# Window attention with a sticky top-1 mixture of experts: first-layer matmuls over five PSUM banks, gathers and a branch hint issued at other places

## The chip, the cores and the metric

The kernel runs on one core of one Trainium2 chip. The core has five engines with an instruction queue each: TensorE (PE, with its weight loads listed as PEld), VectorE (DVE), ScalarE (ACT), GpSimd (POOL, which also issues the indirect DMAs here) and SyncE (SP, which issues the other DMAs). The metric is device time of one execution in microseconds (us); lower is better.

## The reference

Attention comes first: 8 batches, 8 heads, 512 local and 32 global positions. Its rows then go through a mixture of 8 experts. A token takes the expert with the largest logit, or, when its local gate is at least 0.5, the expert of the token before it.

```python
# attention, per batch and head (D = 64, window = 32)
out_g = sm(scale * q_g @ k_all.T) @ v_all                 # 32 global rows see everything
s_ll  = where(|i - j| <= 32, scale * q_l @ k_l.T, -1e9)   # 512 local rows see a band
out_l = sm([scale * q_l @ k_g.T, s_ll]) @ [v_g, v_l]      # and the 32 global keys
x = [out_g, out_l] as (8, 544, 512)
# experts (E = 8, F = 1024), token s of batch b
fresh = argmax(x[b, s] @ w_gate)
e = fresh if s == 0 or sigmoid(x[b, s] @ w_local) < 0.5 else e_of_previous_token
out[b, s] = softmax(x[b, s] @ w_gate)[e] * (relu(x[b, s] @ w1[e]) @ w2[e])
```

## The kernel before, in words

The program has three stretches. Until about 230 us it computes attention batch by batch and writes the rows x, with their gate values and token numbers, into a buffer `xs` in DRAM. From then on it computes experts, in blocks of rows that share one expert. Blocks 0 to 2 ("early", 256 rows each) use only rows of the first batches, and the end of attention and the routing of the last batches (the generator `tail`) run between their instructions. Blocks 3 to 10 ("rem") are one per expert and take what is left of it, in a number of rows known only at run time. Then come "full" blocks of 256 rows, each inside an `If`; three of them run with these inputs.

One block does this. Its rows are gathered from `xs` by indirect DMAs of 128 rows (`gather`, L1182, on POOL) into `xr4` (named `xa` in the trace), transposed on PE (`xpose`, L1196), and split by ACT (L1198) and DVE (L1199) into a high and a low part. The weights come in eight pieces of 128 x 1024 (`load`, L1135, on SP), and ACT (L1145) and DVE (L1155) split each piece in the same way. The first layer (`mm1`, L1242) makes eight groups fc = 0..7, each of 12 matmuls into one PSUM bank. ACT then takes the relu out of that bank (L1244), DVE takes the rest that ACT's rounding left (L1245), and only then is the bank free for another group. The second layer (`mm2`, L1253) adds up 24 matmuls of 512 columns for each 128 rows. `store` scales the result on ACT by a row factor (L1258) and scatters it by an indirect DMA on POOL (L1259). The row factors and token numbers are made on DVE by `scal` (L1208 to L1210), which reads all the gathered rows.

A rem block is a `Switch` over ten arms. Case 0 (`half`) takes 128 rows, with PE's operands exchanged. The other cases (`part`) take n = 256 to 512 columns in steps of 32. In `part` the first layer takes its banks from the ring `ph`, which holds three at that time. After the arm comes the common part, `close`: it stores the last result of the arm, runs the second layer for the last 128 rows, transposes the rows 256 to 511 of the next block, makes that block's scales, and gathers for the block after it. `xr4` is a single buffer, so each gather into it has to wait until `xpose` and `scal` have read what was there. The close of one block and the arm of the next transpose the rows of that next block: the arm the row groups 0 and 1, the close the groups 2 and 3.

Before a Switch a `hint` is issued on every engine: it loads the case number from `cnd` (L1420) and announces the branch (L1426). For the first rem block this stands in early block 2. The case numbers are the last eight small DVE operations of `kinds` (L1048 to L1064). The row lists of the first rem block come from the first `pick`: three DVE operations (L989 to L993), 34 small matmuls on PE (L999), two DVE operations (L1001, L1002), then its four gathers. `pick` waits a number of turns of `tail` between its DVE operations and its matmuls; one turn in two falls to a hook after a group of matmuls.

All engines run in program order, and the order of the program is that of the Python code: `hook` and `step`, called after each group of matmuls, put one or more pieces of the other engines' work at that place.

Of the kernel before, what the change touches and what calls it, by code (L numbers as in the profile page):

```python
# [30 lines left out]
NT = 34  # L31
# [7 lines left out]
NX = 3  # L39
# [550 lines left out]
class Route:  # L590
# [414 lines left out]
    def lists(self, po):  # L1005
        nc = self.nc
        yield from self.place(self.cntp, NT, NX, NR)
        cid = self.tmp("cid", [P, 2 * E + NR, 2], BF16)
# [19 lines left out]
        phi = self.tmp("phi", [P, NT], BF16)  # L1028
# [4 lines left out]
        for c0 in range(CA, NT, 5):  # L1033
            yield from self.low(c0, min(c0 + 5, NT))
        self.pk = (cid, phi)
        yield from self.pick(cid, phi, self.o2, 0, 4, 2 * NX, ((0, NT),), po, 12)

    def kinds(self):
        nc = self.nc
# [31 lines left out]
class Moe:  # L1071
# [100 lines left out]
        e = self.rt.eide[0:1, i:i + 1] if i < NX else self.rt.eid[0:1, i - NX - E:i - NX - E + 1]  # L1172
        return self.nc.sync.value_load(e, min_val=0, max_val=E - 1)

    def gather(self, i):
        if i >= NSLOT:
            return
        k = self.kind(i)
        src = self.xs[0:P * (CA + 1)] if k == "early" else self.xs
        c0 = 2 * i if k == "early" else 2 * NX + 4 * (i - NX) if k == "rem" else 2 * NX + 4 * E + 2 * (i - NX - E)  # L1180
        for j in range(4 if k == "rem" else 2):
            self.nc.gpsimd.indirect_dma_start(out=self.xr[j] if k == "early" else self.xr4[:, j], out_offset=None, in_=src,  # L1182
                                              in_offset=bass.IndirectOffsetOnAxis(ap=self.rt.idx[:, c0 + j:c0 + j + 1], axis=0))

# [44 lines left out]
            self.load()  # L1229
            self.split(True)  # L1230

    def mm1(self, i, fc, xh, xl, hh, hl, n0, n1):
        nc = self.nc
        hi, lo = self.wp[8 * i + fc // 2]
        hi = hi.rearrange("p (c f) -> p c f", c=4)
        lo = lo.rearrange("p (c f) -> p c f", c=4)
        fs = slice(P * (fc % 2), P * (fc % 2) + P)
        ph = self.ph()[:, 0:n1 - n0]
        n = 0
        for a, b_ in ((hi, xh), (lo, xh), (hi, xl)):  # L1240
            for dc in range(4):
                nc.tensor.matmul(ph, a[:, dc, fs], b_[:, dc, n0:n1], start=(n == 0), stop=(n == 11))  # L1242
                n += 1
        nc.scalar.activation(out=hh[:, fc, n0:n1], in_=ph, func=AF.Relu)  # L1244
        nc.vector.scalar_tensor_tensor(out=hl[:, fc, n0:n1], in0=ph, scalar=0.0, in1=hh[:, fc, n0:n1].bitcast(F32), op0=ALU.max, op1=ALU.subtract)  # L1245
# [50 lines left out]
    def early(self, i):  # L1296
# [4 lines left out]
        for fc in range(8):  # L1301
            self.mm1(i, fc, *x, 0, 256)
            self.hook(i, fc)
        self.ph = Ring(self.ph.t[0:n])
        py = self.py()
        for fc in range(8):
# [5 lines left out]
                    self.gather(i + 2)  # L1312
        if mid:
            self.widen()
            self.finish(True)
        self.store(py, 0)
        py = self.py()
        for fc in range(8):
            if mid and fc == 1:
                while not self.known:  # L1320
                    self.take(next(self.tail))
                self.hint(i + 1)
            self.mm2(i, py, fc, 1, *x[2:])
            self.hook(i, 16 + fc)
            if mid and fc in XPM:
                self.xpose(i + 1, XPM.index(fc))
                if fc == XPM[-1]:
                    self.scals(i + 1)
# [45 lines left out]
    def part(self, i, n0, n1, groups):  # L1374
# [2 lines left out]
            for t in self.g:  # L1377
                self.nc.vector.tensor_copy(t[:, 1:2], t[:, 3:4])
        for fc in range(8):
            self.mm1(i, fc, *x, n0, n1)  # L1380
            self.step(fc % 2 == 0, fc != 4)
        for g, j in enumerate(groups):
            last = j == groups[-1] and self.kind(i) == "rem"
# [11 lines left out]
    def close(self, i, j):  # L1395
        py = self.py.t[j % 2]
        if self.kind(i) == "rem":
            self.store(self.ps[7], 1)
        for fc in range(8):
            self.mm2(i, py, fc, j, self.HH, self.HL)  # L1400
            if fc in (2, 5):
                self.xpose(i + 1, 2 + fc // 3)
                if fc == 5:
                    self.scals(i + 1)
                    self.gather(i + 2)
            self.step(fc in (1, 3, 5, 7))
        self.store(py, j)

# [145 lines left out]
```

## Time and profile before

| | us |
|---|---|
| median of three runs | 718.87 |
| lowest, highest | 712.88, 720.37 |
| the profiled execution, whole | 717.19 |
| its span, first to last instruction | 715.4 |
| PE busy | 674.5 (94% of the span) |
| DVE busy | 426.9 (60%) |
| ACT busy | 343.7 (48%) |
| POOL busy | 199.3 (28%) |
| mean granted PE clock | 0.979 |

PE is busy for all but a few places, so what counts is where it stands still and where its granted clock is low. A row of the waits names who waited, who ended it, the sum of the time, the number of times and the longest. A row of the timeline has the start, the duration of the merged group, the engine, line and operation, the tiles written and read, and in brackets the idle time before it and what ended that.

The second and third early block begin their first layers at 268.1 and 296.0 us. The rem blocks begin their arms at 327.3 (480 columns), 372.0 (`half`), 392.8 (352), 433.3 (448), 476.5 (352), 511.3 (288), 543.1 (448) and 586.6 (416). The full blocks begin at 628.0, 651.5 and 674.9.

### The profile page before, as it was taken

The page shows a single profiled execution, that of the slowest core. Times are in us where ns is not written, and L with a number is a line of the kernel's source. Part 1 is how long each engine was busy: PE and PEld are TensorE (multiplying, and loading weights), DVE is VectorE, ACT ScalarE, POOL GpSimd, SP SyncE. Part 2 cuts the span into 40 slices and gives each one's busy share as a digit, 9 for nine tenths or more (in the row PEclk, how much of TensorE's full clock was granted, in tenths as well). Part 3 has the DMA queues.
Part 4 walks back from the last instruction along what each step waited for, and adds up shares of the span by engine and source line. Part 5 has one row for each costly group of instructions (what it writes and reads, how often), then busy time and mean ns, then how long its engine had stood idle before and what let it go on. Part 6 is the DMA issues. An engine that isn't in the chain of part 4 may idle for free. (4 is left out here: it accounts for less than half of the span.)

```text
span 715.4 us, 18380 instructions
## 1 busy us (share of the span) xinstructions
PE 674.5 (94%) x7253; PEld 565.9 (79%) x7253; DVE 426.9 (60%) x1057; ACT 343.7 (48%) x614; POOL 199.3 (28%) x321
## 2 busy tenths in 40 slices
PE   8999999999899999898997799999999999999990
PEld 7777777777677869787886789889888889899880
DVE  7878777778887777893335526335445325166550
ACT  4565555555546646453345435243535334256550
POOL 6634434343343110412023213031303020122201
PEclk9999999999999999999998899999999999999996
DMA  8966876966585676767327727246556326176551
GB/s 330 371 244 238 325 276 236 356 252 224 219 309 178 222 231 234 258 212 279 96 95 260 252 82 239 94 137 212 172 191 206 121 90 198 65 264 236 194 194 50
DMA packets 42869, 150.92 MB, mean 211 GB/s; under 512 B 7950, under 2 KB 9230, under 8 KB 38545
## 3 DMA queue, kind: packets, MB, share of 16 engines
q1 hardware_dynamic: 35392, 126.39, 50.6%
q0 software_dynamic: 6960, 21.90, 8.9%
q8 instruction: 77, 1.26, 0.7%
q14 instruction: 152, 1.24, 0.6%
q10 hardware_dynamic: 288, 0.13, 0.1%
HBM read 130.02 MB, written 19.69 MB: 209 GB/s over the span
## 5 line engine op out<-in xcount | busy, mean ns | idle before, releaser
L1253 PE MATMUL ps<-wp,wq 128*128 128x512 f32 x504 | 128.1, 401 | 0.5 <-ACT wq L1353 0.5
L1259 POOL DMA_INDIRECT out_dram<-y,tk x39 | 48.0, 1232 | 287.7 <-ACT y L1258 259.7
L1242 PE MATMUL ps<-wp,wp 128*128 128x256 f32 (+5 forms) x672 | 110.8, 325 | 3.5 <-issue 2.5
L1242 PEld LDWEIGHTS ps<-wp,wp 128*128 128x128 f32 x672 | 105.0, 191 | 8.9 <-issue 3.9
L1253 PEld LDWEIGHTS ps<-wp,wq 128*128 128x128 f32 x504 | 93.7, 191 | 20.5 <-ACT wq L1353 0.9
L1199 DVE TENSOR_TENSOR wp<-ps,wp 128x512 fp32r<-128x512 f32 x40 | 27.5, 690 | 106.9 <-ACT wp L1198 106.8
L1245 DVE SCALAR_TENSOR_TENSOR wq<-ps,wq 128x256 fp32r<-128x256 f32 (+5 forms) x80 | 41.9, 526 | 80.3 <-ACT wq L1244 67.7
L1244 ACT ACTIVATE wq<-ps 128x256 fp32r<-128x256 f32 (+5 forms) x80 | 37.3, 468 | 84.7 <-PE ps L1242 79.1
L191 POOL TENSOR_SCALAR_AFFINE_SELECT qbd<-raw 64x512 f32<-64x512 f32 x62 | 44.6, 720 | 118.1 <-PE ps L243 98.1
L243 PE MATMUL ps<-kx,qbd 128*64 128x128 f32 x1024 | 70.8, 280 | 0.9 <-issue 0.7
L243 PEld LDWEIGHTS ps<-kx,qbd 128*64 128x64 f32 x1024 | 54.7, 137 | 11.9 <-issue 7.8
L1182 POOL DMA_INDIRECT xa<-xs,idx x42 | 46.6, 1110 | 59.9 <-issue 41.8
L1258 ACT ACTIVATE y<-ps,pp 128x512 f32<-128x512 f32 x39 | 26.9, 690 | 72.9 <-PE ps L1253 66.4
L248 DVE TENSOR_REDUCE mx<-ps 128x4 f32<-128x512 f32 x64 | 43.9, 686 | 26.8 <-PE ps L243 26.7
L1155 DVE TENSOR_TENSOR wp<-raw,wp 128x1024 fp32r<-128x1024 f32 x47 | 57.1, 1217 | 0.0
L254 ACT ACTIVATE pe<-pe 128x512 f32<-128x512 f32 x64 | 40.7, 636 | 30.3 <-DVE pe L250 30.3
L1145 ACT CAST wp<-raw 128x1024 fp32r<-128x1024 f32 x49 | 51.1, 1046 | 4.2 <-DMA raw<-in_w_dram 3.4
L1198 ACT CAST wp<-ps 128x512 fp32r<-128x512 f32 x40 | 23.5, 588 | 58.1 <-PE ps L1196 58.0
L250 DVE TENSOR_TENSOR pe<-ps,mx 128x512 f32<-128x512 f32 x64 | 44.0, 688 | 1.6
L276 PE MATMUL ps<-v,pt 128*32 128x65 f32 x2048 | 42.4, 222 | 2.4 <-DVE xa L284 0.8
L276 PEld LDWEIGHTS ps<-v,pt 128*32 128x32 f32 x2048 | 33.3, 110 | 13.8 <-issue 6.6
L191 POOL TENSOR_SCALAR_AFFINE_SELECT kx<-raw 128x384 f32<-128x384 f32 (+3 forms) x127 | 42.8, 369 | 2.8 <-DMA raw<-in_qk_dram 0.7
(287 smaller groups left out, 1173.3 us busy)
## 6 DMA issues: line engine op xcount, KB each, us to landing
raw<-in_w_dram SPq DMA_DIRECT2D x79, 512.0 KB, 4.3
v<-in_vw_dram SPq DMA_DIRECT2D x32, 1040.0 KB, 9.3
raw<-in_qk_dram SPq DMA_DIRECT2D x32, 528.0 KB, 7.1
xa<-in_w_dram SPq DMA_DIRECT2D x22, 512.0 KB, 4.2
xT<-in_w_dram SPq DMA_DIRECT2D x22, 512.0 KB, 5.7
xs<-xa SPq DMA_DIRECT2D x8, 1056.0 KB, 4.6
qgb<-in_qg_dram SPq DMA_DIRECT2D x8, 128.0 KB, 4.0
xa<-xs,idx POOLq DMA_INDIRECT x42, 5.8
```

Source lines behind the costliest of these rows:

```text
L191: self.nc.gpsimd.affine_select(out=out, in_=in_, pattern=pat, compare_op=ALU.is_ge, fill=0.0, base=0, channel_multiplier=0)
L243: nc.tensor.matmul(sp[64 * t2:64 * t2 + 64, t], qbd[:, w], kf[:, f:f + P], start=False, stop=True, skip_group_check=True)
L248: nc.vector.tensor_reduce(out=mx, in_=st["sp"], axis=AX.X, op=ALU.max)
L250: nc.vector.tensor_tensor(out=st["pe"][:, 4 * hb:4 * hb + 4], in0=st["sp"], in1=mx.broadcast_to([P, 4, P]), op=ALU.subtract)
L276: nc.tensor.matmul(o[32 * w4:32 * w4 + 32, g, h], pt[:, 2 * g + w4 // 2, w4 % 2, h, :], v[:, w, h * (D + 1):(h + 1) * (D + 1)], start=True ...
L1145: nc.scalar.copy(out=hi, in_=raw)
L1155: (nc.gpsimd if pool else nc.vector).tensor_tensor(out=lo, in0=raw, in1=hi.bitcast(F32), op=ALU.subtract)
L1182: self.nc.gpsimd.indirect_dma_start(out=self.xr[j] if k == "early" else self.xr4[:, j], out_offset=None, in_=src, in_offset=bass.IndirectO ...
L1242: nc.tensor.matmul(ph, a[:, dc, fs], b_[:, dc, n0:n1], start=(n == 0), stop=(n == 11))
L1245: nc.vector.scalar_tensor_tensor(out=hl[:, fc, n0:n1], in0=ph, scalar=0.0, in1=hh[:, fc, n0:n1].bitcast(F32), op0=ALU.max, op1=ALU.subtract)
L1253: nc.tensor.matmul(py, a[:, fc, js], b_[:, fs], start=(fc == 0 and k == 0), stop=(fc == 7 and k == 2))
L1259: sc = nc.gpsimd.indirect_dma_start(out=self.out, out_offset=bass.IndirectOffsetOnAxis(ap=self.g[1][:, j:j + 1], axis=0), in_=y, in_offset ...
```

## The change

Four things change.

1. In `part`, the first layer takes the banks 2, 3, 6, 1, 7, 2, 3, 6 for its groups 0 to 7, where it took 2, 3 and 6 in turn.
2. In `close`, the row scales of the next block and the first two gathers for the block after it stand behind the first group of the second layer (they stood behind the sixth); the transposes stand behind the groups 2 and 4 (2 and 5), and the other two gathers behind group 4.
3. The matmuls of the first `pick` come ten turns of `tail` later (a wait of 22 for 12), which is five groups of the first layer of early block 2: they stood ahead of its group 0 and stand ahead of its group 5.
4. In early block 2, `finish(True)`, what is left of `kinds`, and the first hint stand behind the last group of the first layer. `finish(True)` stood behind the second layer's first 128 rows, the rest one group later.

```diff
@@ lists @@
-        yield from self.pick(cid, phi, self.o2, 0, 4, 2 * NX, ((0, NT),), po, 12)
+        yield from self.pick(cid, phi, self.o2, 0, 4, 2 * NX, ((0, NT),), po, 22)
@@ gather @@
-    def gather(self, i):
+    def gather(self, i, part=range(4)):
...
-        for j in range(4 if k == "rem" else 2):
+        for j in part:
+            if j >= 2 and k != "rem":
+                break
@@ mm1 @@
-    def mm1(self, i, fc, xh, xl, hh, hl, n0, n1):
+    def mm1(self, i, fc, xh, xl, hh, hl, n0, n1, bank=None):
...
-        ph = self.ph()[:, 0:n1 - n0]
+        ph = (self.ph() if bank is None else bank)[:, 0:n1 - n0]
@@ early @@
         for fc in range(8):
             self.mm1(i, fc, *x, 0, 256)
             self.hook(i, fc)
+            if mid and fc == 7:
+                self.finish(True)
+                while not self.known:
+                    self.take(next(self.tail))
+                self.hint(i + 1)
...
         if mid:
             self.widen()
-            self.finish(True)
         self.store(py, 0)
         py = self.py()
         for fc in range(8):
-            if mid and fc == 1:
-                while not self.known:
-                    self.take(next(self.tail))
-                self.hint(i + 1)
             self.mm2(i, py, fc, 1, *x[2:])
@@ part @@
-            self.mm1(i, fc, *x, n0, n1)
+            self.mm1(i, fc, *x, n0, n1, self.ps[(2, 3, 6, 1, 7, 2, 3, 6)[fc]])
@@ close @@
-            if fc in (2, 5):
-                self.xpose(i + 1, 2 + fc // 3)
-                if fc == 5:
-                    self.scals(i + 1)
-                    self.gather(i + 2)
+            if fc == 0:
+                self.scals(i + 1)
+                self.gather(i + 2, (0, 1))
+            if fc in (2, 4):
+                self.xpose(i + 1, 1 + fc // 2)
+                if fc == 4:
+                    self.gather(i + 2, (2, 3))
```

The first place is PE's queue in early block 2 around the hint (`cnd` holds the case numbers, `ps_63` and `ps_64` are the banks of the second layer, `ps_65` and `ps_66` banks of the first; behind L1244 and L1255 of the changed kernel stand L1242 and L1253 of the kernel before). Before:

```order
L1253 MATMUL ps_63<-wq_4315,hl 128x512
L1253 MATMUL ps_64<-wq_4314,hh 128x512 x2
L1253 MATMUL ps_64<-wq_4314,hl 128x512
L1420 TENSOR_LOAD cnd
L1426 SWITCH_STRIDE
L1426 ISA
L1426 BRANCH_PREFETCH_HINT
```

After:

```order
L1244 MATMUL ps_65<-xl,wp_4313 128x256 x4
L1244 MATMUL ps_66<-xh,wp_4313 128x256 x8
L1244 MATMUL ps_66<-xl,wp_4313 128x256 x4
L1424 TENSOR_LOAD cnd
L1430 SWITCH_STRIDE
L1430 ISA
L1430 BRANCH_PREFETCH_HINT
L1255 MATMUL ps_63<-wq_4314,hh 128x512 x2
```

The four instructions of the hint have moved from behind nine groups of the second layer to the place between the two layers.

The second place is DVE's queue at the end of the first layer of early block 2 (`hl<-ps` frees a bank of the first layer, `wp<-raw,wp` is a split of weights, `kq`, `kb` and `kt` lead to the case numbers in `cnd`). Before:

```order
L1155 TENSOR_TENSOR wp_100<-raw_77,wp_100 128x1024
L1245 SCALAR_TENSOR_TENSOR hl<-ps_65,hh 128x256
L1055 TENSOR_SCALAR kb<-kq 1x8
L1058 TENSOR_SCALAR kt<-kq 1x8
L1060 TENSOR_TENSOR kt<-kt,kb 1x8
L1245 SCALAR_TENSOR_TENSOR hl<-ps_66,hh 128x256
L1062 SCALAR_TENSOR_TENSOR kt<-left,kt 1x8
L1064 TENSOR_TENSOR cnd<-kt,kb 1x8
L1155 TENSOR_TENSOR wp_101<-raw_78,wp_101 128x1024
L1245 SCALAR_TENSOR_TENSOR hl<-ps_63,hh 128x256
```

After:

```order
L1155 TENSOR_TENSOR wp_4207<-raw_79,wp_4207 128x1024
L1247 SCALAR_TENSOR_TENSOR hl<-ps_66,hh 128x256
L1048 TENSOR_SCALAR kq<-cn 1x8
L1050 TENSOR_SCALAR kq<-kq 1x8
L1052 TENSOR_SCALAR kq<-kq 1x8
L1055 TENSOR_SCALAR kb<-kq 1x8
L1058 TENSOR_SCALAR kt<-kq 1x8
L1060 TENSOR_TENSOR kt<-kt,kb 1x8
L1062 SCALAR_TENSOR_TENSOR kt<-left,kt 1x8
L1064 TENSOR_TENSOR cnd<-kt,kb 1x8
L1424 TENSOR_LOAD cnd
```

The last eight operations of `kinds` stood spread between the groups 2 to 4; they now stand together behind the last group, with the hint right behind them.

The third place is DVE's queue in the common part of the first rem block (`tm_99`, `tk_96` and `pp_93` are the scales and token numbers of the next block, `wp_4311<-ps` the low parts of its transposed rows). Before:

```order
L1420 TENSOR_LOAD cnd
L1426 SWITCH_STRIDE
L1426 ISA
L1426 BRANCH_PREFETCH_HINT
L1199 TENSOR_TENSOR wp_4311<-ps_68,wp_4209 128x4x128
L1155 TENSOR_TENSOR wp_4207<-xa_109,wp_4207 128x1024
L1155 TENSOR_TENSOR wp_4208<-xa_109,wp_4208 128x1024
L1199 TENSOR_TENSOR wp_4311<-ps_67,wp_4209 128x4x128
L1208 TENSOR_TENSOR tm_99<-xa_108,eoh 128x32
L1209 COPY tk_96<-xa_108 128x4
L1210 TENSOR_REDUCE pp_93<-tm_99 128x4
```

After:

```order
L1424 TENSOR_LOAD cnd
L1430 SWITCH_STRIDE
L1430 ISA
L1430 BRANCH_PREFETCH_HINT
L1210 TENSOR_TENSOR tm_99<-xa_108,eoh 128x32
L1211 COPY tk_96<-xa_108 128x4
L1212 TENSOR_REDUCE pp_93<-tm_99 128x4
L1201 TENSOR_TENSOR wp_4311<-ps_68,wp_4209 128x4x128
L1155 TENSOR_TENSOR wp_4207<-xa_109,wp_4207 128x1024
L1201 TENSOR_TENSOR wp_4311<-ps_67,wp_4209 128x4x128
L1155 TENSOR_TENSOR wp_4208<-xa_109,wp_4208 128x1024
```

The three operations of the scales have moved ahead of everything that DVE does with this common part's transposes. POOL's queue keeps its order (store of the arm's last rows, four gathers, store of the common part).

## The prediction

> **What bounds the kernel now.** I read first the page, then PE's waits from 290 us on, because nothing before that is moved, then the timelines around each wait. The page gives the span; PE is busy in nearly all of it.
>
> ```profile
> span 715.4 us, 18380 instructions
> ```
>
> The waits of PE from 290 us to the end, longest sum first:
>
> ```profile
> PE ps L1242 <- DVE wq L1245: 3.9, 2, 3.6
> PE ps L999 <- DVE xT L993: 3.3, 1, 3.3
> PE ps L1196 <- DMA xa<-xs,idx: 3.2, 2, 2.3
> PE ps L1242 <- issue: 2.5, 1, 2.5
> PE ps L1242 <- ACT wp L1145: 0.9, 1, 0.9
> PE ps L1196 <- DVE wp L1199: 0.8, 1, 0.8
> PE ps L1253 <- ACT wq L1353: 0.5, 1, 0.5
> ```
>
> Together they are 15.1 us, and the change aims at three of them: the bank wait of the first layer (3.9), the first pick (3.3), the gathers of the rows after `half` (3.2). The granted clock adds to them. The 3 us behind the wait at the first pick, in the table of stretches (PE, PEld, DVE, ACT and POOL busy, granted clock, share and rate of the DMA engines):
>
> ```profile
> 296.00:299.00 3.00, 3.00 (x19) 3.00 (x16) 2.42 (x4) 0.10 (x1) 2.18 (x2) 0.51 0.91 280
> ```
>
> PE is busy all the time, at half clock. So a standstill of about 3 us costs itself and a slow stretch behind it.
>
> **Early block 2: the first pick and the hint.** PE's timeline there:
>
> ```profile
> 295.10 1.00 PE L999 MATMUL ps<-xT,o 128*128 128x8 bf16 x34 [3.27 <-DVE xT L993]
> 295.96 1.99 PE L1242 MATMUL ps<-xh,wp 128*128 128x256 f32 x8
> ...
> 300.41 1.12 PE L1242 MATMUL ps<-xh,wp 128*128 128x256 f32 x8
> ...
> 309.05 0.62 PE L1253 MATMUL ps<-wq,hh 128*128 128x512 f32 x2
> ```
>
> The six groups 2 to 7 of the first layer run from 300.41 to 309.05, 1.44 us each. Groups 0 and 1 took 4.45 (295.96 to 300.41) where they take 2.88, so the slow clock cost 1.6 us. With the pick gone from ahead of group 0, PE could begin at 295.10 - 3.27 = 291.8. What is late next is DVE:
>
> ```profile
> 294.70 3.49 DVE L1155 TENSOR_TENSOR wq<-raw,wq 128x1024 fp32r<-128x1024 f32 x3
> ...
> 303.16 0.32 DVE L1048 TENSOR_SCALAR kq<-cn 1x8 int32<-1x8 int32 x1
> ...
> 303.79 1.21 DVE L1155 TENSOR_TENSOR wp<-raw,wp 128x1024 fp32r<-128x1024 f32 x1
> ...
> 305.26 0.15 DVE L1055 TENSOR_SCALAR kb<-kq 1x8 f32<-1x8 int32 x1
> ...
> 305.60 0.41 DVE L1245 SCALAR_TENSOR_TENSOR hl<-ps,hh 128x256 fp32r<-128x256 f32 x1
> ```
>
> In its queue three weight splits stand ahead of the first L1245, and they run until 298.2 whatever PE does. The early blocks keep three banks, so groups 0 to 2 run from 291.8 to 296.1 and group 3 waits until 298.2 + 0.4 = 298.6. Of the 3.27 us, 2.5 return as a bank wait. Then groups 3 and 4 end at 301.5, the pick (0.9, from 295.10 to 295.96) at 302.4, groups 5 to 7 at 306.7, where before they ended at 309.05: 2.3 us won.
>
> But now the hint stands here, and PE loads the case number that DVE must first make. Group 6 ends at 305.3; relu and L1245 (0.2 + 0.4 + 0.4) bring 306.3, three small operations 306.6, the split that now stands ahead of group 7's L1245 (1.2) 307.8, that L1245 308.2. The eight operations of the case numbers took 0.63 us for the first three (303.16 to 303.79), 0.34 for the next three (305.26 to 305.60) and about 0.3 for the last two: `cnd` at 309.5. The relu's 0.4 is that of this row, which begins 0.2 after PE:
>
> ```profile
> 309.25 0.39 ACT L1244 ACTIVATE hh<-ps 128x256 fp32r<-128x256 f32 x1 [1.05 <-PE ps L1242]
> ```
>
> No row shows a hint on an empty PE queue. Its price lies between 0 (before, it was hidden among the matmuls) and the 2.5 that PE spent at the first Switch with nothing to wait for (its wait "issue"). I take 0.5, PE's wait at L1253 after `half`, where a jump and a hint also stand behind a drained queue. So the second layer begins at 310.0, 1.0 later than before. PE has then stood for 3.3 us, and I count one stretch at half clock, 1.6 us as after the old wait. That lets DVE catch up, so its 0.8 at L1196 goes: +1.8 us by the first Switch. The 2.5 there I leave as it is: the 34 short matmuls still drain PE's queue right before it, and how much an announcement 15 us ahead instead of 9 helps is shown nowhere (0 to 2.5 won). Bounds of the whole place: -2.8 (hint free, no half clock, Switch wait gone) and +7.4 (hint 2.5, half clock after both standstills, 1.6 and 2.9, the latter the dearest in the trace, from the next part). I stay in the middle because of PE's two standstills one, 2.5 us, is shorter than the old 3.27, and the other, 3.3, as long.
>
> [...]
>
> The first gathers start about 4 us later than before (after L1002 at about 303, which was at 298.3), but their rows are needed first at 318; they took 6 us, so 0.
>
> **The block after `half`.** PE, ACT, DVE and POOL:
>
> ```profile
> 384.37 4.10 PE L1253 MATMUL ps<-wp,wq 128*128 128x512 f32 x9 [0.52 <-ACT wq L1353]
> ```
>
> ```profile
> 378.95 1.06 ACT L1145 CAST wp<-raw 128x1024 fp32r<-128x1024 f32 x1
> ...
> 389.68 0.69 ACT L1258 ACTIVATE y<-ps,pp 128x512 f32<-128x512 f32 x1 [5.35 <-DMA out_dram<-y,tk]
> ```
>
> ```profile
> 380.72 0.69 DVE L1199 TENSOR_TENSOR wp<-ps,wp 128x512 fp32r<-128x512 f32 x1
> ```
>
> ```profile
> 373.46 1.35 POOL L1182 DMA_INDIRECT xa<-xs,idx  x1 [5.67 <-PE ps L1362]
> ...
> 380.14 1.42 POOL L1259 DMA_INDIRECT out_dram<-y,tk  x1 [0.31 <-ACT wp L1145]
> ```
>
> `half` is short, and the gathers, issued from 373.46 on, land after PE wants them. With the scales first on DVE the first two gathers are issued 5.4 us earlier, when the store ahead of them is done (about 368), and both waits of L1196 end. But the win is not 3.2 us plus the rest: ACT is busy with a weight cast until 380.0 and takes the first transposed rows only then, DVE's part of them begins at 380.72 and ends at 381.4, and the last transposes of `half` need their bank. They can start at about 381.5; with 0.9 for them and ACT's copy, the second layer begins at 382.4 instead of 384.37: -2.0. PE still stands mostly idle ahead of that, so I leave the slow clock (up to 1.8 more if it goes: nine matmuls took 3.9 us here, and 2.1 at 0.234 each, a third of 0.70, the usual group of three).
>
> Then the next first layer, of 352 columns:
>
> ```profile
> 392.83 4.08 PE L1242 MATMUL ps<-wp,hh 128*128 128x352 f32 x24
> 396.75 2.08 PE L1242 MATMUL ps<-wp,hl 128*128 128x352 f32 x12
> 402.47 3.89 PE L1242 MATMUL ps<-wp,hl 128*128 128x352 f32 x12 [3.64 <-DVE wq L1245]
> 406.15 9.00 PE L1242 MATMUL ps<-wp,wp 128*128 128x352 f32 x48
> ```
>
> ```profile
> 401.89 0.52 DVE L1245 SCALAR_TENSOR_TENSOR wq<-ps,wq 128x352 fp32r<-128x352 f32 x1 [5.06 <-issue]
> ```
>
> DVE reaches this arm at 396.8 (401.89 - 5.06) and stands 5.06 us with nothing that the profile shows to wait for; I take it for code that isn't there yet. PE fills three banks and stops. Five banks carry PE to 392.8 + 5 x 1.96 = 402.6, and DVE frees the first at 402.4 (401.89 + 0.52). Besides, the store at 380.14, which waited behind four gathers, goes out near 374, so ACT's 5.35 at the `y` buffer shrinks, and DVE gets through the common part sooner. Either alone nearly ends the stop. The layer took 22.3 us (392.83 to 406.15 + 9.00); 96 matmuls at the pace of the first 24, 3.92 us, are 15.7: -6.6, of which 3.6 is the wait and 2.9 the slow clock behind it. Bounds: -2.0 for the whole part (DVE's code later still, the stop returns) and -10.4.
>
> The other arms never waited for a bank but for 0.2 us (516.5 us): -0.2. Bank 7 is read by the store at the beginning of the common part and bank 1 by one at its end, 0.7 us long; groups 4 and 3 come at least 4.3 us (three groups) later, so the new banks cost 0; if ACT came later than that, PE would wait for what is left.
>
> **The end.** POOL issues the last two gathers, which nobody needs, ahead of the last store:
>
> ```profile
> 698.48 0.69 ACT L1258 ACTIVATE y<-ps,pp 128x512 f32<-128x512 f32 x1 [1.07 <-PE ps L1253]
> ```
>
> ```profile
> 700.83 1.02 POOL L1259 DMA_INDIRECT out_dram<-y,tk  x1 [0.30 <-issue]
> ```
>
> Now they start when the store before them is out (694.9) and need 2.6 us, so the last store starts 0.4 after `y`, at 699.5: -1.3 (between -0.5 and -1.5). In the other common parts POOL has 4 to 25 us of slack; the moved scales, transposes and gathers cost 0 under PE's 24 matmuls. Were DVE to wait there for a late gather, the transposes behind the scales would be late with it.
>
> **Sum.** +1.8 - 2.0 - 6.6 - 0.2 - 1.3 = -8.3. The profiled execution took 717.19 (span 715.4), so 708.9. It lies 1.7 below the median of the runs shown, 718.87, so against that median the forecast is -1.4%.
>
> **Rivals.** About 1% is what a measurement of this kernel can tell from no change.
>
> *The cover is not there (25%).* DVE's 5 us without a reason are no fault of the gathers; if the shorter `half` gives the hint less time before the Switch, DVE comes later by as much as PE wins. Then the part is worth -2.0, the sum -1.7, the time 715. For it: ACT's waits have "issue" too, behind other Switches. Against it: five banks and an earlier DVE both have to fail.
>
> *The hint stops PE (7%), slower.* `cnd` may come later than 309.5, since each of the splits ahead needs its weights: a landing 2.4 us later than the usual 4.2 (the slowest load of that stretch took 6.6) moves it to 311.9; a hint on an empty queue as dear as DVE's 5.06 moves the second layer to 317.0; with 2.9 for the clock that is +10.9, less 0.8. With the part after `half` at its -2.0 and the end at -1.3 the time is 724. It decides for slower once early block 2 loses more than the 10 us that the other parts win; against it, that no PE row shows more than 2.5 without a reason.
>
> *It pays in full (8%).* No half clock at either place, and the earlier hint ends the 2.5: -2.8 - 10.4 - 0.2 - 1.3 = -14.7, 702.5.
>
> The forecast itself has 60%. The predicted time is 709, and the forecast's own range 705 to 712. For 8 in 10 I take 704 to 717. Faster by over 1% (under 711.7) are the forecast nearly whole and the full pay: 0.64. Within 1%: 0.29. Slower: 0.07.
>
> **What would show it.** Right: L999 in early block 2 without a wait and instead about 2.5 us of PE waiting for L1245 at group 3; PE idle about 3 us between the layers with the case numbers ending it; no wait of L1196 for a gather in `half`; no wait for a bank in the block behind it, even if DVE still stands without a reason; the last store within 0.5 us of its `y`. Wrong: a PE wait of over 4 us at the hint, or the bank wait still there with five banks, or new PE waits in the common parts of the eight rem blocks.

## The result, and the profile after

The changed kernel takes 711.12 us (median of 13 runs, 709.32 to 715.48), the kernel before in the same series 717.33 us (13 runs). The ratio is 0.9916, with a 95% interval of 0.9892 to 0.9941: 0.84% faster, where 1.4% was forecast. That 1.4% was taken against 718.87, the median of three runs; against 717.33 the predicted 709 us is 1.2% less. The profiled execution took 711.1 us with a span of 709.4, 6.0 less than before.

These are PE's waits from 285 us on in the changed kernel, longest sum first. The lines are numbered two higher than before (L1255 is the second layer, L1244 the first, L1198 the transposes):

```profile
PE ps L1255 <- issue: 4.1, 1, 4.1
PE ps L1244 <- DVE hl L1247: 2.5, 1, 2.5
PE ps L1353 <- DVE wp L1201: 1.1, 1, 1.1
PE ps L1255 <- ACT wq L1355: 1.0, 1, 1.0
PE ps L1244 <- issue: 0.7, 1, 0.7
PE ps L1244 <- ACT wp L1145: 0.7, 1, 0.7
PE ps L1198 <- DVE wq L1356: 0.6, 1, 0.6
```

All three waits that the change aims at are gone (3.9, 3.3 and 3.2 us). Two new ones stand at the top, both in early block 2.

**Early block 2.** PE's timeline: the beginning of the first layer, its fourth group (group 3), the first pick, the beginning of the second layer, the second pick and the first arm:

```profile
293.57 1.12 PE L1244 MATMUL ps<-xh,wp 128*128 128x256 f32 x8
...
300.52 1.22 PE L1244 MATMUL ps<-xh,wp 128*128 128x256 f32 x8 [2.48 <-DVE hl L1247]
...
304.70 1.10 PE L999 MATMUL ps<-xT,o 128*128 128x8 bf16 x34
...
314.27 1.22 PE L1255 MATMUL ps<-wq,hh 128*128 128x512 f32 x2 [4.05 <-issue]
...
331.95 8.37 PE L1244 MATMUL ps<-wp,wp 128*128 128x480 f32 x38 [0.67 <-issue]
```

The first layer begins at 293.57, 1.74 later than it could before (291.83), though nothing ahead of it differs: that is scatter of the execution (it lies between 291.8 and 294.1 in the kernels of this study), and is taken off below. The pick itself (L999) no longer waits. Group 3 waits 2.48 for the bank instead, and the groups 3 and 4 took 4.18 together (300.52 to 304.70) where two take 2.88. The second layer waits 4.05. The first arm begins 38.4 us behind the first layer (293.57 to 331.95); before it was 35.5 (291.83 to 327.30).

DVE's timeline up to the end of the hint:

```profile
311.35 0.15 DVE L1048 TENSOR_SCALAR kq<-cn 1x8 int32<-1x8 int32 x1
...
312.83 0.15 DVE L1064 TENSOR_TENSOR cnd<-kt,kb 1x8 int32<-1x8 f32 x1
314.17 0.67 DVE L989 TENSOR_TENSOR xT<-cid,phi 128x486 bf16<-128x486 bf16 x1 [1.19 <-issue]
```

The case numbers are ready at 312.98 (312.83 + 0.15). DVE goes on 1.19 later and PE 1.29 later: both had the hint to get through, with nothing queued ahead of it. The stretches behind the two standstills (PE, PEld, DVE, ACT and POOL busy, granted clock, share and rate of the DMA engines):

```profile
302.13:305.13 3.00, 3.00 (x27) 2.91 (x27) 0.56 (x2) 1.56 (x3) 0.00 (x0) 0.50 1.01 395
...
315.00:318.00 3.00, 3.00 (x9) 2.33 (x8) 2.97 (x5) 1.97 (x3) 0.00 (x0) 0.50 0.30 75
318.00:319.00 1.00, 1.00 (x4) 0.81 (x3) 0.96 (x3) 0.00 (x0) 0.00 (x0) 0.50 0.83 332
319.00:321.00 2.00, 2.00 (x10) 1.57 (x10) 1.97 (x4) 0.00 (x0) 0.00 (x0) 0.99 0.16 66
```

Each standstill is followed by half clock: some 3 us of it behind the first, and from 314.27 to 319 behind the second. The length of the second is that of this execution. Two other kernels of this study have the same order of work up to there ("Pick and hint moved, alone" and "Four output buffers"). They stand 4.04 and 4.05 us at the hint too, but their half clock is over by 316.6, and the first arm begins 38.3 and 37.5 us behind the first layer. In the first of them:

```profile
317.00:319.00 2.00, 2.00 (x10) 1.63 (x9) 1.93 (x5) 0.00 (x0) 0.00 (x0) 1.00 0.58 229
```

**The block after `half`.** PE's timeline, from the last wait inside `half` to the next first layer:

```profile
385.96 0.44 PE L1353 MATMUL ps<-idf,gsb 128*128 128x128 f32 x2 [1.08 <-DVE wp L1201]
387.37 3.86 PE L1255 MATMUL ps<-wp,wq 128*128 128x512 f32 x9 [0.98 <-ACT wq L1355]
395.59 4.09 PE L1244 MATMUL ps<-wp,hh 128*128 128x352 f32 x24
399.52 4.00 PE L1244 MATMUL ps<-wp,hl 128*128 128x352 f32 x24
403.36 7.84 PE L1244 MATMUL ps<-wp,wp 128*128 128x352 f32 x48
```

No transpose waits for a gather, and the first layer of 352 columns runs through in 15.6 us (395.59 to 411.20), where it took 22.3. The nine matmuls behind `half` are still at half clock (3.86; 0.50 granted from 387.3 to 390.7). ACT and DVE at the beginning of the common part behind `half`:

```profile
392.32 0.69 ACT L1260 ACTIVATE y<-ps,pp 128x512 f32<-128x512 f32 x1 [5.52 <-PE ps L1198]
```

```profile
392.59 0.19 DVE L1210 TENSOR_TENSOR tm<-xa,eoh 128x32 f32<-128x32 f32 x1 [4.20 <-issue]
```

ACT stands as long as before (5.52, was 5.35), and DVE stands 4.20 beside it.

**The end.** ACT and POOL:

```profile
694.16 0.69 ACT L1260 ACTIVATE y<-ps,pp 128x512 f32<-128x512 f32 x1 [1.07 <-PE ps L1255]
```

```profile
695.13 1.02 POOL L1261 DMA_INDIRECT out_dram<-y,tk  x1 [0.51 <-ACT y L1260]
```

The last store starts 0.28 behind its `y` (694.85), where 1.66 lay between them (699.17 to 700.83).

The account of the profiled execution: +1.7 scatter, +2.9 early block 2, -1.9 `half` up to its next arm (20.8 to 18.9), -6.7 the first layer behind it, -1.4 the end. That is -5.4 of the -6.0.

### The profile page after: what moved, and what is told of

It reads as the page before. It is cut to its first block, busy times and chain, and to the rows that moved or that the text cites. A ratio compares the mean times of both kernels' runs of the same rounds, so it can differ in the third digit from the quotient of the medians.

```text
span 709.4 us, 18373 instructions
## 1 busy us (share of the span) xinstructions
PE 673.1 (95%) x7253; PEld 563.9 (79%) x7253; DVE 429.1 (60%) x1057; ACT 343.7 (48%) x614; POOL 202.2 (28%) x321
## 3 DMA queue, kind: packets, MB, share of 16 engines
q14 instruction: 149, 1.22, 0.6%
## 4 chain that ended last, share of the span: by engine, by line
PE 57%; DVE 4%; issue 1%; SPq 1%; ACT 1%; DMA 1%; POOL 0%; POOLq 0%; ACTq 0%; DVEq 0%
PE ps L1255 28%; PE ps L1244 25%; PE ps L1198 2%; DVE wq L1155 1%; PE ps L1364 1%; DMA raw<-in_w_dram 1%; SPq L417 0%; PE ps L999 0%; DVE wp L1155 0%; DVE hl L1247 0%; POOL xa L1184 0%; DVE o L905 0%; DVE xl L1201 0%; PE ps L276 0%; ACT hh L1246 0%
## 5 line engine op out<-in xcount | busy, mean ns | idle before, releaser
L1261 POOL DMA_INDIRECT out_dram<-y,tk x39 | 44.4, 1140 | 317.5 <-ACT y L1260 297.9
L1255 PE MATMUL ps<-wp,wq 128*128 128x512 f32 x504 | 128.0, 401 | 1.0 <-ACT wq L1355 1.0
L1244 PE MATMUL ps<-wp,wp 128*128 128x256 f32 (+5 forms) x672 | 109.3, 323 | 1.3 <-issue 0.7
L1255 PEld LDWEIGHTS ps<-wp,wq 128*128 128x128 f32 x504 | 93.6, 190 | 20.6 <-ACT wq L1355 1.2
L1244 PEld LDWEIGHTS ps<-wp,wp 128*128 128x128 f32 x672 | 103.7, 189 | 6.4 <-issue 1.9
L1260 ACT ACTIVATE y<-ps,pp 128x512 f32<-128x512 f32 x39 | 26.9, 690 | 78.1 <-PE ps L1255 71.4
L1184 POOL DMA_INDIRECT xa<-xs,idx x42 | 53.2, 1266 | 19.7 <-issue 10.0
```

What stands on the lines that cost most here:

```text
L1255: nc.tensor.matmul(py, a[:, fc, js], b_[:, fs], start=(fc == 0 and k == 0), stop=(fc == 7 and k == 2))
L1261: sc = nc.gpsimd.indirect_dma_start(out=self.out, out_offset=bass.IndirectOffsetOnAxis(ap=self.g[1][:, j:j + 1], axis=0), in_=y, in_offset ...
```

## The experiments

Every kernel below is timed against the kernel before, on the same chip and in the same series; each ratio is to that, and kernels of different series are compared by their ratios. The "stretch" is the time from where PE could begin the first layer of early block 2 to the first arm. In the five kernels of this study in which the first pick stands at its old place (the kernel before among them) it is 33.9 to 35.9 us, so only a difference of more than 2 us is more than scatter. Each stretch is read from one execution.

### Five banks alone

```diff
-            self.mm1(i, fc, *x, n0, n1)
+            self.mm1(i, fc, *x, n0, n1, self.ps[(2, 3, 6, 1, 7, 2, 3, 6)[fc]])
```

> The kernel before with the five banks alone. Theory: PE's 3.6 us at the third bank behind the half block and the 2.9 us of slow clock after it go, although DVE still comes late, while the waits for the gathers in the half block (3.2 us) and the end stay: 6 to 6.6 us less than before, ratio 0.991. Rival (the banks only move the stop, DVE's lateness decides): the bank wait returns at the sixth group, under 2 us less, ratio above 0.997.

Measured: 711.59 us, ratio 0.9912 (0.9881 to 0.9944). PE's waits for gathers and its first layer behind `half`:

```profile
PE ps L1196 <- DMA xa<-xs,idx: 3.2, 2, 1.7
```

```profile
394.49 4.08 PE L1242 MATMUL ps<-wp,hh 128*128 128x352 f32 x24 [0.53 <-ACT wp L1198]
398.40 4.00 PE L1242 MATMUL ps<-wp,hl 128*128 128x352 f32 x24
402.24 7.84 PE L1242 MATMUL ps<-wp,wp 128*128 128x352 f32 x48
```

The gathers still come late, yet the layer takes 15.6 us without a wait. The banks by themselves end the stop.

### Moved scales and gathers alone

```diff
-            if fc in (2, 5):
-                self.xpose(i + 1, 2 + fc // 3)
-                if fc == 5:
-                    self.scals(i + 1)
-                    self.gather(i + 2)
+            if fc == 0:
+                self.scals(i + 1)
+                self.gather(i + 2, (0, 1))
+            if fc in (2, 4):
+                self.xpose(i + 1, 1 + fc // 2)
+                if fc == 4:
+                    self.gather(i + 2, (2, 3))
```

> The kernel before with the moved scales, transposes and gathers of the common part alone, three banks. Theory (either part alone ends most of the stop): half block 1.7 to 2.0 us less, end 1.3 to 1.7 less, and the bank wait of the next first layer falls from 3.6 to about 0.6 us without a slow clock, 5 us or more less: together 7.5 to 9, ratio 0.988 to 0.990. Rival (the five banks are needed): half block and end alone, 3 to 3.7 us less, ratio about 0.995, with the bank wait still at 3 us or more.

Measured: 711.43 us, ratio 0.9936 (0.9906 to 0.9967). PE's first layer behind `half`, with three banks:

```profile
392.50 4.08 PE L1244 MATMUL ps<-wp,hh 128*128 128x352 f32 x24 [0.38 <-ACT wp L1200]
396.42 2.08 PE L1244 MATMUL ps<-wp,hl 128*128 128x352 f32 x12
399.67 2.19 PE L1244 MATMUL ps<-wp,hl 128*128 128x352 f32 x12 [1.18 <-DVE wq L1247]
401.70 7.84 PE L1244 MATMUL ps<-wp,wp 128*128 128x352 f32 x48
```

The bank wait falls from 3.64 to 1.18, and no half clock follows (the 12 matmuls behind it took 2.19, before 3.89): 17.0 us (392.50 to 409.54) for 22.3. So each of the two parts nearly ends the same stop, as the prediction has it. PE has the first bank back 7.17 us behind the layer's beginning here (392.50 to 399.67), where it was 9.64 before (392.83 to 402.47): with the moved scales and gathers DVE comes there sooner. The time is not what the theory said, 5.5 us less (7.5 to 9 were expected), and its ratio lies nearer to the rival's 0.995. In the trace `half`, the layer and the end win 10.1 us, but the first arm loses 1.8: there PE stood 2.46 at the Switch, as before (2.45), and this time the 96 matmuls behind it took 22.75, where they took 20.91.

### Pick and hint moved, alone

```diff
-        yield from self.pick(cid, phi, self.o2, 0, 4, 2 * NX, ((0, NT),), po, 12)
+        yield from self.pick(cid, phi, self.o2, 0, 4, 2 * NX, ((0, NT),), po, 22)
...
+            if mid and fc == 7:
+                self.finish(True)
+                while not self.known:
+                    self.take(next(self.tail))
+                self.hint(i + 1)
...
```

> The kernel before with the later first pick and the earlier hint alone. Theory: this pair loses time, about 2.9 us from the start of early block 2's first layer to the arm of the first rem block (a bank wait of 2.5 and a wait of 4 at the hint for the 3.3 that goes, the Switch wait 1.8 shorter): ratio 1.002 to 1.006. Rival (the pair is a gain, the loss seen in the changed kernel is upstream drift): 1 to 4 us less, ratio below 0.999.

Measured: 717.65 us, ratio 1.001 (0.9993 to 1.0027); no measurable difference. The loss of 0.2 to 0.6% that was expected is not shown by the time, though the interval reaches into it; the gain of the rival is ruled out. PE's waits:

```profile
PE ps L1253 <- issue: 4.0, 1, 4.0
PE ps L1242 <- DVE wq L1245: 3.4, 2, 2.5
PE ps L1196 <- DMA xa<-xs,idx: 2.6, 2, 1.4
PE ps L1242 <- DVE hl L1245: 2.4, 1, 2.4
```

The two new waits stand there as in the changed kernel (4.0 and 2.4), and the stretch is 38.3 us. The time shows less of it (+0.8 us) than the stretch does: in this trace the old waits behind `half` were a little shorter, 2.5 for 3.6 at the bank and 2.6 for 3.2 at the gathers. So the pair gains nothing by itself.

### Banks and moved gathers without pick and hint

This is the changed kernel with its third and fourth part (the pick, the case numbers and the hint) taken back.

> The changed kernel without the moved pick and hint (five banks and moved gathers alone). Theory: 2.5 to 3.5 us less than the changed kernel, 707.5 to 708.5 us, ratio to before 0.986 to 0.988. Rival (the pair is neutral or a gain): at the changed kernel's 711 or above, ratio 0.991 or more.

Measured: 708.47 us, ratio 0.9892 (0.9865 to 0.9919); its stretch is 34.3 us, where the changed kernel's is 38.4. Together the two parts win 1.08%, apart 0.88% and 0.64%. The overlap, 0.44% or some 3 us, fits the stop that either ends, but each of the three has an interval of 0.3% to each side. In the traces it is plain: the layer behind `half` took 22.3 us, and takes 15.6 with the banks, 17.0 with the moved gathers and 15.6 with both. Without pick and hint the kernel is faster than with them by 2.65 us (medians of two series) or 1.7 us (0.24%, by the ratios). The intervals of the two ratios overlap (0.9892 to 0.9941 with them), so the time alone doesn't prove it. The stretches do: 37.5 to 38.4 us in the three traces with the late pick and the hint between the layers, 33.9 to 35.9 in the five with the pick at its old place.

### The early hint with the pick at its old place

The changed kernel with 12 again for 22: the pick stands ahead of group 0, the hint behind group 7.

> Five banks, moved gathers and the early hint, but the first pick where it was. Theory (the wait at the hint is the price of the two together, because the later pick puts the case numbers behind the last group of the first layer): the case numbers are made 2 to 3 us before PE comes to the hint, so PE waits under 1.5 us there for the load of the number alone, and the wait at the first Switch is about 1 us shorter: 707.5 to 709.5, as without the pair. Rival (the hint between the layers costs by its place): a wait of about 4 us, 711.

Measured: 707.84 us, ratio 0.9881 (0.9846 to 0.9916). PE's waits:

```profile
PE ps L999 <- DVE xT L993: 3.1, 1, 3.1
PE ps L1244 <- issue: 2.3, 2, 1.9
PE ps L1198 <- DVE wp L1201: 1.7, 1, 1.7
```

PE doesn't wait for the hint at all: the case numbers are done at 306.7, the second layer begins at 309.49. It is the later pick that pushed them behind the last group, because `tail` yields its pieces in order and the case numbers come behind the pick. The stretch is 35.7 us. The wait at the first Switch did not shorten, though the announcement stands as early as in the changed kernel: PE still stands 1.94 there (1.92 with pick and hint both at their old places).

```profile
328.15 8.17 PE L1244 MATMUL ps<-wp,wp 128*128 128x480 f32 x36 [1.94 <-issue]
```

### The hint inside the second layer

The pick stays late; the hint moves behind the fourth group of the second layer.

```diff
             if mid and fc == 7:
                 self.finish(True)
-                while not self.known:
-                    self.take(next(self.tail))
-                self.hint(i + 1)
...
             self.hook(i, 8 + fc)
+            if mid and fc == 3:
+                while not self.known:
+                    self.take(next(self.tail))
+                self.hint(i + 1)
```

> The changed kernel with the first hint behind the fourth group of early block 2's second layer, where its case numbers are long made; the pick stays late. Theory (DVE's queue of weight splits and list operations bounds this stretch, PE only waits at other places): the 4 us at the hint and the slow clock behind it go, but PE then waits about 2 us at the third transpose for DVE, and the stretch from the first layer of early block 2 to the first rem arm takes about 35 us as in the kernel before instead of 38.4: 2 to 4 us less than the changed kernel, 707 to 709, ratio to before 0.986 to 0.989. Rival (PE's own waits are the price, and all of it comes back): 6 us less, 705.

Measured: 705.64 us, ratio 0.9849 (0.982 to 0.9877). This interval lies wholly below the changed kernel's: a version that beats both kernels. The time is the rival's (705), and below the theory's 707 to 709. PE behind the hint:

```profile
313.59 0.80 PE L1255 MATMUL ps<-wq,hh 128*128 128x512 f32 x2 [2.29 <-DVE xT L991]
```

Four groups of the second layer were to cover the hint, and they did not quite: the case numbers came at 312.31, because DVE's splits stand ahead of them, and PE still stood 2.29. The profile names another DVE operation there; PE went on 1.28 behind the case numbers, as in the changed kernel. The stretch is 35.9 us, as the theory has it. But this execution took 708.05 us, the longest of the six, with a mean granted clock of 0.981 where the other five have 0.989 to 0.991. So the trace shows more half clock than this kernel mostly has, and whether its usual stretch is 35.9 us too is not shown.

### The late pick with the hint at its old place

The changed kernel with the early hint alone taken back.

> The changed kernel with the late first pick, but with the case numbers and the first hint where they stood before the change. Theory (only the place of the hint costs; the late pick itself gives about 2 us less the bank wait that DVE leaves): no wait of PE at L1255 behind the hint, the bank wait at group 3 of early block 2 stays 2.3 to 2.6 us, the wait at the Switch is back near 2 us because the announcement comes some 9 us ahead of it instead of 15; time within 1.5 us of the kernel with the hint inside the second layer (705.6), that is 704.5 to 707.5 when the kernel before is at 716. Rival (DVE is what binds the whole stretch, so any place of the pick gives the same): the waits only change their names, and the time is that of the kernel without pick and hint moved, 708 to 709.

Measured: 709.14 us, ratio 0.9903 (0.987 to 0.9937). The theory missed; the rival had it. PE's waits, and PE at the transposes ahead of the Switch:

```profile
PE ps L1198 <- DVE wp L1201: 3.3, 1, 3.3
PE ps L1244 <- DVE hl L1247: 2.3, 1, 2.3
```

```profile
323.38 1.12 PE L1198 MATMUL ps<-idf,xa 128*128 128x128 f32 x4 [3.34 <-DVE wp L1201]
```

```profile
328.82 7.50 PE L1244 MATMUL ps<-wp,wp 128*128 128x480 f32 x33
```

Nothing waits at the hint and nothing at the Switch (the last row is the first arm, without a wait), but PE stands 3.34 at the transposes, since DVE reaches them no earlier: 29.9 us behind the start of the stretch, 29.7 with the hint inside the second layer. The stretch is 36.0 us. PE's waits have changed their names. In all the kernels with DVE's work unchanged and three banks, whatever the order, the stretch is 33.9 us or more.

### Five weight splits on POOL

The kernel with the hint inside the second layer, with five of DVE's splits in and behind early block 2 given to POOL.

```diff
-            self.split()
+            self.split((i, k) in ((1, 17), (1, 19), (2, 10), (2, 12), (2, 14)))
```

> As the kernel with the hint inside the second layer, and five weight splits of this stretch (two ahead of the first layer of early block 2, three in its second layer) on POOL, which is idle there, instead of DVE: DVE has 6 us less to do, POOL takes about 2.4 us for each. Theory (DVE bounds the stretch): the bank wait of 2.5 us and the wait at the third transpose go, the stretch falls from 35 to 29 to 32 us: 702 to 706. Rival (PE, or the landing of the weights, bounds it): within 1 us of the kernel with the hint inside.

Measured: 718.02 us, ratio 1.0021 (0.9994 to 1.0048); both theories missed. DVE, and POOL beside it:

```profile
295.38 5.27 DVE L993 TENSOR_SCALAR xT<-xT,ipf 128x136 bf16<-128x136 bf16 x1
```

```profile
295.87 4.70 POOL L1155 TENSOR_TENSOR wq<-raw,wq 128x1024 fp32r<-128x1024 f32 x2
```

A DVE operation that takes 0.53 elsewhere took 5.27: it ended only when POOL's two splits did (at 300.65, they at 300.57). What was taken from DVE's queue came back as a stall of DVE, and PE's bank wait rose to 4.9. The other three splits met the same: beside each of them a DVE operation of 0.15 to 0.67 took 2.3 to 2.7. This run says nothing on whether DVE binds the stretch.

### Five weight splits left out

The same five splits done by nobody: the low parts of five pieces of weights keep what the buffer held, so this part of the computation is missing. The weight load that follows each of them goes out a little earlier with it.

> The kernel with the hint inside the second layer, with five of DVE's splits of weights in early block 2 and behind it left out (the low parts of those five pieces stay what they were, so the output is not the reference's): 6 us less work on DVE in a stretch of 36 us from the first layer of early block 2 to the first arm. Theory (DVE binds the stretch): the bank wait at group 3 and the wait at the hint go, the clock stays high, and the stretch falls to 30 to 32 us, one run near 701. Rival (PE's own work, the code behind the branch and the gathers bind it): the bank wait goes, but the stretch stays over 34 us.

Measured: 702.5 us in one run. The stretch is 31.9 us, 4.0 less than in the trace with the splits, which was that kernel's longest execution; the time is 3.1 less than its median (705.64). The rows of PE behind its only long wait, and the clock there:

```profile
311.25 0.72 PE L1255 MATMUL ps<-wq,hh 128*128 128x512 f32 x2 [2.77 <-DVE xT L989]
```

```profile
311.00:312.00 1.00, 0.75 (x3) 0.68 (x4) 0.96 (x3) 0.88 (x1) 0.00 (x0) 1.00 0.91 351
312.00:313.00 1.00, 1.00 (x6) 0.77 (x5) 0.77 (x2) 1.00 (x2) 0.00 (x0) 1.00 0.76 272
```

The bank wait is gone and the clock stays at 1.00, as the theory has it; the wait at the hint stays, which it hadn't. DVE had no pause from 303.2 to the case numbers at 310.05 even so. So at most 4.0 us come out for the 6.1 taken from DVE's queue (five splits of 1.22). How much of that is DVE's work as such, and how much the bank wait and the half clock behind it, this run alone does not show; the next one bears on it.

### A fourth bank in early block 2

The kernel with the hint inside the second layer, the ring of the first layer one bank longer there.

```diff
-        self.ph = Ring(self.ph.t + [self.py.t[self.py.k % 2]])
+        self.ph = Ring(self.ph.t + [self.py.t[(self.py.k + d) % 2] for d in range(2 if mid else 1)])
```

> The kernel with the hint inside the second layer, and a fourth bank for the first layer of early block 2. Theory (DVE's queue of splits binds the stretch from the first layer to the first arm): the 2.4 us bank wait at group 3 shrinks to under 1 us, but what is won there comes back as a wait later in the stretch (at the hint, at the transposes or at the Switch); time within 1 us of the kernel with three banks there (705.6). Rival (the bank wait and the slow clock behind it are lost by themselves): the stretch is 2.5 to 4 us shorter and the time 702 to 703.

Measured: 705.29 us, ratio 0.9856 (0.9813 to 0.99). PE at the bank and at the hint:

```profile
298.79 1.22 PE L1244 MATMUL ps<-xh,wp 128*128 128x256 f32 x8 [0.78 <-DVE hl L1247]
...
310.78 0.72 PE L1255 MATMUL ps<-wq,hh 128*128 128x512 f32 x2 [2.22 <-DVE xT L989]
```

Inconclusive. The bank wait is 0.78 for 2.39, and in the trace nothing of it comes back: the stretch is 33.0 us, 3.0 shorter, as the rival has it. The time is that of three banks (705.64) within 0.4 us, as the theory has it. The two ratios have intervals of 2 and 3 us to each side, so they can't tell 3 us apart; and the traces compare the longest of six executions with three banks (708.05) with one below the median with four (704.51). What the traces do show is that DVE's queue is not of a fixed length. With all its work it reaches the transposes 26.9 us behind the start here, for 29.7. In the first layer DVE itself waits for relus out of PE's groups, 1.8 us here and 4.1 with three banks, where PE runs at half clock from 300.5 to 303.8. This trace, with all splits, comes within 1.1 us of the one with five left out.

### Four output buffers

The changed kernel with a ring of four `y` for three, to see whether ACT's wait behind `half` was one for a free `y`.

> The changed kernel with four buffers for the scaled results instead of three. ACT stands 5.5 us at the first store behind the half block. Theory 1 (it waits for the scatter out of its buffer): the wait goes. Theory 2 (the code behind the jump out of the arm is not there yet, as DVE stands 4.2 us at the same place): it stays at 4 to 6 us.

Measured: 711.16 us in one run. ACT:

```profile
391.43 0.69 ACT L1260 ACTIVATE y<-ps,pp 128x512 f32<-128x512 f32 x1 [5.83 <-PE ps L1198]
```

The wait stays. It is not the buffer.

## Why the prediction was right, and where it was not

The sign and the main gain hold. For the profiled execution -8.3 us was forecast and -6.0 came, +1.7 of scatter among it; by the medians it is -6.2, and 711.12 lies near the slow end of the forecast's range of 705 to 712. By its own steps:

- **The first layer behind `half`, -6.6: right,** in size (22.3 to 15.6 us) and in kind. Five banks do it with the gathers still late; the moved gathers leave 1.18 of the wait without the banks. The rival "The cover is not there" is out on both counts: five banks cover DVE's lateness, and DVE came no later with the scales and gathers moved. Its pause is 2.31 us in the changed kernel, 5.06 before; with them moved alone PE had the first bank back 7.17 us behind the layer's beginning, where it was 9.64 before and 8.49 with pick and hint alone.
- **ACT's wait at `y` shrinks: wrong.** The prediction took the 5.35 for a store that goes out late and let it add to the cover. The store did go out earlier, ACT stood 5.52 all the same, and a fourth `y` changed nothing. DVE stands at the same place, 4.20 without a wait that the profile shows, and it has such a pause at the first operation of six of the other seven common parts of the rem blocks, 3.1 to 3.3 us: this is the first work behind a jump out of an arm. Whether the code was not there yet (the prediction's reading of DVE's 5.06) is not shown: the trace has DMA packets of instructions (queues q8 and q14) in that pause, seven from 388.9 to 392.6 us where the whole execution has 226, but not for which engine, and no run tried the jump itself. By what way the moved scales and gathers bring DVE sooner to the next arm (its pause there is 2.31, was 5.06) is not shown either. The step cost nothing in the sum, since the banks cover the wait alone.
- **`half` itself, -2.0: right** (-1.65 to the second layer). Both waits for gathers went, and behind them stood the weight cast of ACT and DVE's part, as written; the slow clock stayed in this trace, as written. It does not always: in the nine other kernels with the moved gathers the block takes 17.7 to 20.4 us to the next arm, and its nine matmuls 2.31 to 4.20, by how much half clock the execution has there.
- **The end, -1.3: right** (-1.4), the last store 0.28 behind `y`.
- **The new banks cost 0: right.** No arm waits for one.
- **Early block 2, +1.8: the sign right, the size too small.** It is +2.9 in the profiled execution (38.4 for 35.5), and 1.7 to 2.65 by the times of the kernels with and without it, whose intervals overlap. The failing step is the chain that leads to the second layer at 310.0. With the scatter taken off, that began at 312.5. Of the 2.5 us, 1.3 is half clock behind the bank wait of group 3, which was priced at nothing because 2.5 is shorter than 3.27; 0.4 is the case numbers, whose eight operations took 1.63 (311.35 to 312.98) and were put at 1.27 from rows in which they stood apart; 0.8 is the hint on an empty queue, 1.29 where 0.5 was taken from another place. Behind that, half clock from 314.27 to 319 cost 2.4 (half of 4.7) and was put at 1.6; in the two other traces with this code it cost about 1.6 and 1.4, so this term was sized well. On the other side the Switch, left at 2.45, fell to 0.67. That 1.8 hides most of the miss, and it is luck: the prediction tied such a gain to the earlier announcement, but with the early hint and the old pick PE stood 1.94 there, and with the old hint and the late pick not at all. In the kernels that leave the splits alone the wait is 1.6 to 2.5 us with the old pick and 0 to 1.1 with the late one, wherever the hint stands; why is not shown.
- **The bank wait of 2.5 at group 3 in place of the pick: right to the row** (2.48), and so was its reason, the splits in DVE's queue.

The prediction named a PE wait of over 4 us at the hint as a sign against it. It came, at 4.05. The rival "The hint stops PE" was thus right that PE would stand there over 4 us, and wrong on the cause and the price. The case numbers came at 311.2 without the scatter, near its 311.9, but not for weights that landed late: DVE's waits on the way there are all for relus out of PE's groups, and of the 1.7 us behind the forecast 1.3 is the half clock in the first layer. The hint cost 1.29, not 5.06, so the place lost 2.9 us and not 10.

The length of a standstill alone did not decide in these traces whether half clock follows. It came behind 2.48 here, and behind 2.22 in the kernel with four banks (granted 0.50 from 313 to 315 us); 2.77 with five splits left out was followed by 1.00. What else does is not shown.

## What to carry to other kernels

A wait that is taken from one engine's queue is won only as far as the engine that it waited for has time to spare: where DVE's queue ends at the same time, PE's wait gets a new name and place (here 2.48 us for a bank in place of 3.27 for the pick). Nor is that queue a fixed length: it may itself wait for a PE that runs at half clock behind a standstill (4.1 us of such waits with three banks, 1.8 with four). Work that another engine must first produce, like a branch hint's number, belongs behind enough queued matmuls to cover both its lateness and the hint's own latency (1.2 to 1.3 us here), and moving one piece of an ordered stream moves everything behind it. Two cures for one stop don't add up (0.88% and 0.64% apart, 1.08% together); time each alone before paying for both. And a trace is one execution: see where its time lies among the runs before you compare its parts.

## What the runs showed of the hardware

- **A hint with nothing queued ahead of it cost PE 1.2 to 1.3 us.** From the end of the case numbers to PE's next matmul: 1.29 in the changed kernel, 1.29 with pick and hint alone, 1.28 with the hint inside the second layer, 1.20 with four banks, 1.20 with the splits left out. DVE pays the same in the changed kernel (1.19). How much of it is the load here and how much the announcement behind it is not shown.
- **Half clock after standstills of less than 2.5 us,** and not after each: behind 2.22 and 2.48 it came (0.50 granted), behind 2.77 (one run) it did not (1.00). At the first Switch the same length went both ways: behind 2.45 in the kernel before the clock stayed at 1.00 (327 to 336 us), behind 2.46 with the moved gathers alone the arm's 96 matmuls took 22.75 us for 20.91. Up to PE's last matmul the traces of the kernels before and after have six slow stretches from 230 us on: three last 3.4 to 3.5 us (from 296.0 before, from 301.9 and 387.3 after), three twice that, 6.9 (from 381.3 and 401.8 before, from 312.2 after). The one from 296.0 cost 1.6 us (4.45 for 2.88). Inside `half`, in the kernels with the moved gathers, the same three short waits of PE (0.60, 1.08 and 0.8 to 1.1 us) were followed by nine matmuls in 2.31 to 4.20 us; so the time of a single execution moves. In the kernel with four banks, behind 2.22:

```profile
313.00:314.00 1.00, 1.00 (x4) 0.81 (x3) 0.96 (x3) 0.00 (x0) 0.00 (x0) 0.50 0.17 67
```

- **DVE operations stood still beside POOL's splits of 128x1024.** 0.53 became 5.27 beside POOL's 4.70 for two splits, and 0.15 to 0.67 became 2.3 to 2.7 beside each of the three later ones (one trace). Why is not shown.
